# Six first-layer banks by exact parts instead of four, with shared small tiles and a finer written order

## The chip, the cores and the metric

The kernel runs on one core of a Trainium2 chip. The metric is the device time of one execution in microseconds (us). Engines: PE is TensorE, DVE is VectorE, ACT is ScalarE, POOL is GpSimd and SP is SyncE (which here only starts transfers).

## The reference

A gated linear attention with outer-product states (4 batches, 8 heads, 768 tokens, 48 features a head), and behind it a two-layer network with a leaky activation. All in float32.

```python
f = 1.0 / (1.0 + np.exp(-f_logit))
for t in range(S):
    state = f[:, :, t, :, None] * state + np.einsum('bhd,bhe->bhde', k[:, :, t], v[:, :, t])
    y[:, :, t] = np.einsum('bhd,bhde->bhe', q[:, :, t], state)
x = y.transpose(0, 2, 1, 3).reshape(B * S, H * D)      # 3072 x 384
h = x @ w_in                                            # 384 x 2048
g = np.maximum(h, 0.0) + alpha * np.minimum(h, 0.0)
out = g @ w_out                                         # 2048 x 384
```

## The kernel before

**Tiling.** Work goes in 12 steps: 6 chunks of 128 tokens by 2 pairs of sequences. A step holds the attention of two sequences on one chunk and the network of those 256 tokens. The attention of step n+1 runs beside the network of step n.

**Attention of a step.** Transfers bring f, q, k, v (`loaded`, lines L313 and L323; POOL's queue after the first step). ACT takes the sigmoid and copies; DVE makes products of gates inside four-token quads (`lagged_all`, L338 to L345), two scans of 289 columns over the quads' gates (`scanned_all`, L373 and L374), and scaled keys and queries. PE makes three kinds of scores: `raw` inside quads (L582), `qu` between quads of a 32-token block (L591), `off` between blocks (L566). DVE copies the first two under masks into `ad` (`lags` L599 and `quartered` L451), for sequence u = 0 and 1 each; ACT places `ad` into the score matrix A (`placed`, L606). PE then makes py = A and state by v (`summed`, L614), and the state's increments (L539). The scaled keys ks are turned by DVE and two SP transfers through DRAM into ksn (L467, L473, L475). ACT copies py into y, and SP transfers carry y through DRAM into xT, features by tokens (`given`, L503 and L505).

**Network of a step.** The first layer has 8 banks f = 0 to 7, each 256 of the 2048 hidden features by 256 tokens, accumulated in one PSUM bank out of a pool of four. A plain bank is `products(f, w_in, xT)` in float32. From step 3 on, banks 3 to 6 are made by parts: w_in is split once into a high part that a float32r pass multiplies exactly and a low part, xT each step likewise. The bank is then a pass hi by xh and a pass lo by xl (word Na), a scaling copy in place on ACT (Nq, L844), and a third pass sum by xs (Nb). xh is a rounding copy on ACT; xl and xs are copies on ACT that POOL transfers finish by adding (words NY and NZ, L823). Each bank ends in ACT's L854 (Nr) and two DVE instructions L859 (Nc), which write `gate`. The second layer is seven half-size products (Np, L886) of sums of gate blocks (L880) with sums of w_out blocks, as in Strassen's scheme; DVE and ACT add their results into o, SP stores it.

**Parts of w_in.** Per piece of w_in in banks 3 to 6: Y is ACT's high part (L770), Z is DVE's low part and sum (L774, L775), and `turnover` (T) scales the four sums on ACT (L796) once the room of the first pieces is free.

**Order.** Tile pools place buffers and put in the semaphores; the order in which PE, DVE and ACT get their instructions is written by hand in `ORDER_WORDS`: a word is a step number and a part, as `4U0`, and issues all instructions of that part at once. SP's and POOL's instructions are ordered by the framework. Small words: f, F, g, G, h, i, k, l, t are stages of the attention's gates, keys and queries; r and u are the score products, R and U the masked copies, A the placing, y and Y the product py and its copy, X the way to xT, d, D and M the state. Matmuls without use (I, J and the first 14, L935) run in the first step.

The constants: masks `mraw` (four shifted copies) and `mquad`, a 1 and 0 pattern `ones` of 289 columns, the gate row `fs` with its separating ones, `ad` for two sequences, `vs` with 16 spare columns for each sequence's rows.

Of the kernel before, what the change touches and what calls it, by code (L numbers as in the profile page):

```python
# [18 lines left out]
C = 128  # L19
# [16 lines left out]
SPLIT = 3, 7  # L36
TURNED = 3
# [4 lines left out]
0e 1e 0I0 0f 0F 0G 0g 0r1 0h 0i 0m 0p 0j 0r0 0I1 0l 0I2 a0 0R0 0I3 0I4 0I5 0q 0o a1 0k a2 0O 0s 0t w0 0u0 0U0 0R1  # L42
0K0 0H0 1f 0J0 0J1 0J2 w1 0K1 0u1 0J3 0U1 1F 0A0 0d 0D 0H1 0A1 w2 1G 0J4 0J5 0y0 0Y0 b0 0J6 0y1 0x0 0Y1 0M 1g 1i 0J7
1r0 0x1 1R0 0X a3 1h a4 b1 w3 a5 1m 1r1 w4 1j 0Na0 v0 0Nr0 0Na1 0Na2 1R1 0Na3 a6 0Nc0 w5 0Nr1 0Na4 0Na5 0Nc1 2e 0Nr2
1l 1k 0Nr3 a7 0Nc2 1o b2 0Nr4 1K0 1p 1O v1 w6 w7 0Na7 1K1 0Nc3 0Nc4 b3 v2 b4 0Na6 1q 0Nr5 0Nc5 1u0 0Nr6 b5 0Nc6 0Nr7
v3 1u1 1s 2f 1U0 0Nc7 b6 1U1 1H0 1A0 2F 1t 0Np0 v4 0Np1 0Np2 v5 1d b7 v6 V 1H1 1D v7 2g 0Np3 0Np4 1A1 1y0 1y1 1Y0
0Np5 W0 1Y1 1X W1 Y3 W2 0Np6 W3 2G 1Na0 W4 W5 0Np7 0No0 2h 1M 0No1 2i 1Nr0 1Na1 Y4 Y5 1Na3 2p 1Nr1 2q W6 1Na2 1Na4
Y6 3e 1Nr2 2u0 2l 1Nc0 1Nr3 2t 1Nc1 2k 1Nm0 1Nr4 1Nc2 2r0 1Nc3 W7 1Nm1 1Na5 1Nc4 1Na6 1Nr5 2R0 1Nr6 2r1 2U0 2K Z3
2u1 1Nc6 2R1 2A0 1Na7 1Nr7 1Nc5 2o 1Np0 2U1 2O 3f 1Nc7 2d Z4 1Nk 2D 2A1 1Np2 3F 1Np1 2y0 2y1 1Np3 2Y0 2Y1 2X 1Nu0
1Nu1 1Nv0 3G 3g 1Np4 1Nd 1Nv1 1Nw0 1Ng 2M 1Nw1 1Ne 1Nj 1Nh 1Np5 3h 1Np6 1Nf 1Nl 3p 1Ni 3i 1NL 2Na0 3l 4e 2Nr0 2Na1  # L50
2Nr1 2Na3 2Na2 1Ns1 3q 2Nr2 3r0 3u0 2Nc0 2Nr3 3k 3t 2Nc1 2Nm0 3R0 3U0 2Na5 2Nc2 2Nc3 2Nm1 2Na4 Z5 2Nr4 3r1 2Nr5 3K
3u1 2Na7 3R1 2Na6 3o 3A0 2Nc5 2Nr6 2Nc4 3O 3U1 2Nc6 Z6 3A1 3d 3D 2Np0 2Nr7 2Np1 2Nk 2Nc7 4f 2Nd T 3y0 3y1 4F 3Y0
2Np2 1Ns0 3Y1 3M 4g 2Np3 4r0 2Nu1 2Nu0 2Np4 3X 2Nv0 4G 2Nv1 2Nw0 2Ng 3Nx 3Ny 2Nw1 2Ne 2Nj 2Nh 2Np5 4h 2Np6 2Nf 2Nl
4p 3Na1 3Nz 3Na0 4i 3Nr0 2NL 2Ni 4k 4l 3NY 3Na2 4q 3Nr1 3Na7 4K 3Na3 5e 2Ns1 3Nr2 3Nc0 3NZ 3Na4 3Nc2 4t 3Nc1 3Nr7
3Nm0 4u0 3Nc7 4R0 4U0 3Nq3 3Na6 4r1 4A0 4R1 3Na5 4u1 4U1 3Nq4 3Nq5 3Nq6 4o 4O 3Nb3 3Nr3 3Nc3 3Nb4 3Nm1 2Ns0 3Nb6
3Nb5 4d 3Nr4 3Nr5 4D 3Np0 4A1 3Nr6 3Nc6 3Nc5 4y0 3Nc4 4y1 3Np2 5f 4M 4Y0 4Y1 3Np1 3Nk 5F 4X 5g 3Np3 3Nu0 3Nu1 3Nv0
5G 3Nv1 3Nw0 3Ng 3Np4 4Nx 4Ny 3Nw1 3Nd 3Ne 5h 3Nj 3Np5 3Np6 3Nh 3Nf 3Nl 5p 3Ni 5r0 4Nz 4Na0 5i 4Nr0 4Na1 3NL 5k 4NY
4Na5 5l 4Nq5 4Na2 5q 4Nr1 5K 4Na3 4Nc0 4Nr2 5u0 5t 4Nc1 4Nm0 4Nc2 5R0 5U0 4Na7 4Nr7 4NZ 4Na4 6e 3Ns1 5r1 4Nc7 4Nq4
4Nq3 5A0 5u1 5R1 5U1 4Na6 4Nb5 4Nb3 5o 4Nq6 4Nr3 5d 5O 4Nc3 4Nb4 5A1 4Nm1 5D 4Nr4 4Nr5 4Nb6 4Np0 4Nr6 5y0 4Nc4 4Nc5
6f 4Nc6 5y1 5Y0 6F 4Np2 5Y1 5X 6g 4Nk 4Np1 4Np3 4Nu0 4Nu1 4Nv0 4Nv1 4Ng 6G 5Nx 5M 4Nw0 4Np4 5Ny 4Nw1 4Nd 3Ns0 4Ne 6h  # L60
4Nj 4Nh 4Np5 4Nf 4Nl 6p 4Ni 5Nz 5Na0 4Np6 6i 5NY 6k 5Nr0 5Na1 4NL 6l 5Na2 6q 5Na7 5Nr1 6t 5Nc1 6u0 5Nr2 5Nc0 6r0
5Nm0 5Nc2 6R0 5Nr7 5NZ 7e 4Ns1 5Na4 6K 5Na3 6U0 5Nc7 5Na5 6r1 5Nq3 6A0 6u1 6R1 6U1 5Nq4 5Nb3 5Nq5 5Na6 5Nb4 6o 5Nr3
5Nq6 5Nc3 6O 6A1 6d 5Nm1 5Nb6 6D 5Nb5 5Nr4 5Nr5 5Np0 5Nr6 5Nc4 5Nc6 7f 6y0 5Nc5 5Nk 7F 6y1 6Y0 5Np2 6Y1 5Np1 6X 7g
5Np3 5Nu0 5Ng 7G 5Nu1 5Nv0 5Nv1 5Nw1 5Np4 6Nx 5Nw0 5Nd 6M 5Ne 6Ny 7h 5Nj 5Nh 5Np5 5Nf 5Np6 4Ns0 7p 5Ni 6Nz 6Na0 5Nl
7i 7l 6NY 6Nr0 6Na1 5NL 7k 7q 6Na2 6Nr1 7t 6Nc1 6Nr2 6Nc0 6Na7 6Nm0 7K 6Na3 6Nq3 7r0 6Nc2 7u0 7R0 6Nr7 6NZ 6Na4 8e
5Ns1 7U0 6Nc7 6Nq4 6Na5 7u1 7r1 6Nq5 7A0 7R1 7U1 6Na6 6Nq6 6Nb3 6Nr3 6Nc3 6Nb4 6Nm1 6Nb6 6Nb5 7A1 7o 6Nr4 6Nr5 6Nc4
6Nr6 7d 8f 6Np0 7O 6Nc5 7D 6Nk 6Np1 7y0 8F 7y1 6Nc6 7Y0 6Np2 7Y1 7X 8g 7Nx 7M 6Np3 6Nu0 6Nu1 6Np4 6Nv0 6Nd 6Nv1 6Nw0
6Ng 8G 7Ny 6Ne 6Nj 6Nw1 8h 6Nh 6Np5 6Nf 7NY 6Np6 5Ns0 6Nl 8p 6Ni 8i 7Nz 7Na0 7Nr0 7Na1 7Nr1 6NL 8k 8l 7Na2 8t 8r0
7Nr2 7Nc0 8q 7Nc1 8R0 9e 6Ns1 8K 7Na3 7Nm0 7Na7 8u0 7Nc2 7Nr7 7NZ 7Na4 8U0 7Na5 7Nq3 7Nq4 7Nc7 8r1 8u1 7Nq5 8A0 7Na6
8R1 7Nb4 7Nb3 8U1 7Nq6 7Nr3 7Nc3 7Nm1 7Nb6 7Nb5 8o 8A1 8d 7Nr4 7Nr5 7Nc4 7Nr6 8D 8O 9f 7Np0 7Nc5 7Nk 7Np1 7Nc6 8y0  # L70
9F 8y1 8Y0 8Y1 7Np2 8X 9g 7Nd 8M 7Np3 7Nu0 7Nu1 8Nx 7Ne 7Np4 7Nv1 7Ng 9G 8Ny 7Nv0 7Nw0 7Nw1 7Np5 7Nh 9h 7Nf 7Nj 9r0
7Np6 6Ns0 7Nl 9p 7Ni 9R0 8Nz 8Na0 8Na7 9i 8Nr0 8Na1 7NL 9k 9l 8Na2 9q 8Nr1 8NY 8Nr2 9t 8Nc0 8Nc2 8Nc1 8Nr7 8NZ 8Na4
# [11 lines left out]
9Ns0 10Nl 10Ni 11Nz 11NY 11Na0 11Nr0 10NL 11Na2 11Nc0 11Na3 10Ns1 11Nr1 11Nc1 11Nm0 11Nr2 11Nc2 11Nr7 11NZ 11Na4  # L84
11Na5 11Nq3 11Nq4 11Na6 11Nq5 11Nb3 11Nc7 11Nq6 11Nb4 11Nr3 11Nb5 11Nc3 11Nr4 11Nr5 11Nm1 11Nb6 11Np0 11Nc4 11Nr6
11Nc5 11Nc6 11Nk 11Np1 11Np2 11Nd 11Np3 11Nu0 11Nu1 11Nv0 11Nv1 11Np4 11Nw0 11Ng 11Ne 11Nw1 11Np5 11Nj 11Nh 11Np6
10Ns0 11Nl 11Nf 11Ni 11NL 11Ns1 11Ns0
"""

def flat():  # L90
# [924 lines left out]
```

## Time and profile before

| what | value |
|---|---|
| median of three runs | 595.62 us (595.44 to 600.27) |
| profiled execution, first to last instruction (span) | 592.1 us |
| profiled execution's whole time | not listed; the median lies 3.5 us above its span |
| PE busy before 42.7 us | 35.8 us |
| PE busy from 42.7 to 556.7 us | 512.4 of 514.0 us |
| PE busy in the last 35.4 us | 31.9 us |
| one DVE gated product L859, one scaling copy L844 | 0.476 us, 0.574 us |
| one score copy L606 (four for a sequence) | 0.403 us |
| one scan L373 | 0.755 us |
| one high part L770, one low part L774 | 0.84 us, 0.95 us |
| POOL's adding transfers L823, issue to landing | 4.0 us |

The profile's page gives each engine's busy time and share, then forty equal slices in tenths, then the chain of work that ended last. Groups are named by the kernel's line and by output <- inputs. PE's records overlap one another, so the cost of one in a run is its start to the next start. The steps' first layers begin at 188.6 us (step 3), 234.7, 281.7, 324.1, 369.7, 416.2, 461.7 and 506.4 us (step 10).

### The profile page before, as it was taken

What the parts mean: (1) busy time and instruction counts of PE and PEld (TensorE: products, weight loads), DVE (VectorE), ACT (ScalarE), POOL (GpSimd) and SP (SyncE); (2) the same over time, 40 slices, a digit from 0 to 9 for tenths busy, and PEclk for the clock granted to TensorE, in tenths of its full rate; (3) what the DMA queues carried; (4) which work ended last, traced back from release to release, by engine and by line L of the source; (5) the groups of instructions that cost most, each with busy time, mean ns of one, the idle gap of its engine ahead of it and who ended that gap; (6) DMA issues with size and microseconds to landing.
All of it is one profiled execution on the core that took longest, in us unless ns stands there. A gap on an engine that the chain in (4) does not pass through costs nothing.

```text
span 592.1 us, 18853 instructions
## 1 busy us (share of the span) xinstructions
PE 580.1 (98%) x8200; PEld 527.9 (89%) x8200; DVE 505.7 (85%) x1027; ACT 300.4 (51%) x561; POOL 68.4 (12%) x114
## 2 busy tenths in 40 slices
PE   8799999999999999999999999999999999999997
PEld 6678767899899999999999999899899999899997
DVE  7889799899999989899989889989989979966243
ACT  5697973461472473483382374374275355443230
POOL 9110010000101101111111101101100100100100
PEclk9689999999999999999999999999999999999999
DMA  9959212612523823724624614722732731611300
GB/s 299 356 160 348 98 22 63 172 30 86 123 86 91 191 78 89 172 65 105 169 60 106 153 68 106 164 74 85 148 110 81 152 110 54 112 44 30 80 2 27
DMA packets 69443, 67.57 MB, mean 114 GB/s; under 512 B 44688, under 2 KB 58640, under 8 KB 69360
## 3 DMA queue, kind: packets, MB, share of 16 engines
q1 hardware_dynamic: 59744, 37.16, 22.1%
q0 software_dynamic: 8880, 28.84, 19.2%
q8 instruction: 64, 1.05, 0.7%
q10 hardware_dynamic: 736, 0.37, 0.2%
q14 instruction: 19, 0.16, 0.1%
HBM read 44.99 MB, written 13.50 MB: 99 GB/s over the span
## 4 chain that ended last, share of the span: by engine, by line
PE 80%; issue 10%; DMA 4%; ACT 3%; DVE 3%; POOL 1%; POOLq 0%; ACTq 0%; DVEq 0%
PE ph L831 36%; PE pa L886 9%; PE pd L886 5%; PE pf L886 5%; PE pe L886 5%; PE pb L886 5%; PE pc L886 4%; PE py L614 3%; PE qu L591 3%; PE raw L582 3%; DMA w_out_raw<-in_w_out 2%; PE pd L539 1%; PE off L566 1%; DVE ad L451 1%; DMA f<-in_fT 1%
## 5 line engine op out<-in xcount | busy, mean ns | idle before, releaser
L831 PE MATMUL ph<-xT,w_in_sb 128*128 128x256 f32 x612 | 137.1, 380 | 0.2 <-DMA xT<-y 0.2
L831 PEld LDWEIGHTS ph<-xT,w_in_sb 128*128 128x128 f32 x612 | 115.1, 190 | 16.9 <-issue 0.9
L854 ACT ACTIVATE gate<-ph 128x512 f32<-128x512 f32 x96 | 54.6, 594 | 134.4 <-PE ph L831 127.5
L859 DVE SCALAR_TENSOR_TENSOR gate<-gate,om,ph 128x256 f32<-128x256 f32 x192 | 81.0, 476 | 25.6 <-ACT gate L854 25.1
L886 PE MATMUL pa<-w_out_sb,gate 128*128 128x192 f32 x352 | 61.7, 329 | 0.0
L880 DVE TENSOR_TENSOR gate<-gate 128x512 f32<-128x512 f32 x88 | 57.6, 690 | 3.2 <-PE pb L886 2.4
L886 PEld LDWEIGHTS pa<-w_out_sb,gate 128*128 128x128 f32 x352 | 57.1, 190 | 0.5
L599 DVE COPY_PREDICATED ad<-mraw,raw 128x256 f32<-128x256 int32 (+1 forms) x96 | 42.7, 445 | 8.9 <-PE raw L582 6.2
L451 DVE COPY_PREDICATED ad<-mquad,qu 128x224 f32<-128x224 int32 (+6 forms) x140 | 42.2, 302 | 6.8 <-PE qu L591 1.7
L606 ACT COPY A<-ad 32x256 f32<-32x256 f32 x96 | 38.7, 403 | 11.8 <-DVE ad L451 10.4
L440 DVE TENSOR_TENSOR scores<-scores,fs 128x768 f32<-128x768 f32 (+5 forms) x60 | 37.4, 623 | 1.6
L844 ACT ACTIVATE ph<-ph 128x512 f32<-128x512 f32 x36 | 20.2, 574 | 34.0 <-PE ph L831 25.2
L831 PE MATMUL ph<-xh,hi 128*128 128x256 f32 x216 | 34.4, 295 | 0.0
L831 PE MATMUL ph<-xl,lo 128*128 128x256 f32 x216 | 32.0, 283 | 0.3 <-issue 0.3
L886 PE MATMUL pb<-t,gate 128*128 128x192 f32 x176 | 31.2, 331 | 0.0
L831 PEld LDWEIGHTS ph<-xh,hi 128*128 128x128 f32 x216 | 28.7, 190 | 2.8 <-issue 1.6
L424 ACT COPY A<-q 48x512 f32<-48x512 f32 x44 | 27.2, 617 | 7.8 <-DVE q L398 7.2
L886 PE MATMUL pd<-t,gate 128*128 128x192 f32 x176 | 30.7, 328 | 0.3 <-DVE gate L880 0.3
L886 PE MATMUL pc<-t,gate 128*128 128x192 f32 x176 | 30.6, 327 | 0.0
L886 PE MATMUL pf<-w_out_sb,gate 128*128 128x192 f32 x176 | 30.5, 327 | 0.0
L323 POOL DMA_DIRECT2D vs<-in_v x22 | 13.2, 605 | 149.4 <-PE py L614 149.1
L886 PE MATMUL pe<-w_out_sb,gate 128*128 128x192 f32 x176 | 30.4, 326 | 0.0
(153 smaller groups left out, 1044.0 us busy)
## 6 DMA issues: line engine op xcount, KB each, us to landing
w_out_raw<-in_w_out SPq DMA_DIRECT2D x8, 767.8 KB, 9.6
w_in_raw<-in_w_in SPq DMA_DIRECT2D x8, 767.2 KB, 9.5
q<-in_qT POOLq DMA_DIRECT2D x11, 512.0 KB, 5.1
f<-in_fT POOLq DMA_DIRECT2D x11, 512.0 KB, 5.2
k<-in_kT POOLq DMA_DIRECT2D x11, 512.0 KB, 4.2
turned<-f SPq DMA_DIRECT2D x40, 128.0 KB, 4.4
ksn<-turned SPq DMA_DIRECT2D x10, 512.0 KB, 3.5
out<-o SPq DMA_DIRECT2D x24, 192.0 KB, 1.9
```

The source lines that it names most:

```text
L424: nc.scalar.copy(A[halves(cc)[1], :, par * HP:(par + 1) * HP, CH * cc:CH * (cc + 1)], x["q3"][rows(par)].rearrange("p (u h c) s t -> p u h ...
L440: nc.vector.tensor_tensor(by_four(us[:, :, UO[m]:UO[m] + 4 * n]), by_four(us[:, :, skip:skip + 4 * n]), spread(fq[:, :, 1:1 + n], n), ALU. ...
L451: nc.vector.copy_predicated(ad[:, u, :, :, 4 * m:DB], mquad[:, lo:lo + n].bitcast(I32).unsqueeze(1).unsqueeze(1).broadcast_to((128, 2, HP, ...
L582: nc.tensor.matmul(raw[DB * j:DB * (j + 1), par, hp * C:hp * C + QW], lhsT=x["k"][r_, g * DB:(g + 1) * DB], rhs=qd[r_, g], start=True, sto ...
L599: nc.vector.copy_predicated(adu[:, :, :, d:4], mraw[:, d, :, d:4].bitcast(I32).unsqueeze(1).broadcast_to((128, H, NB, n)), rv[:, :, QO[d]: ...
L606: nc.scalar.copy(A[s_, u, :, s_], ad[s_, u].rearrange("p r h t -> p (r h) t"))
L831: nc.tensor.matmul(banks[f][:, j * T:(j + 1) * T], lhsT=of[:, kt, 128 * j:128 * (j + 1)], rhs=by[:, kt], start=first_ and kt + j == 0, sto ...
L844: nc.scalar.activation(banks[f], banks[f], AF.Copy, scale=1.0 - 1.0 / EPS)
L854: nc.scalar.activation(to, of, AF.Relu, scale=-1.0)
L859: nc.vector.scalar_tensor_tensor(to[:, j], to[:, j], om[:, m:m + 1], of[:, j], ALU.mult, ALU.add)
L880: nc.vector.tensor_tensor(block(to)[:, p], block(x_)[:, p], block(y_)[:, p], op)
L886: nc.tensor.matmul(banks[to][:, 0:DH], lhsT=block(of)[:, f], rhs=of_w_out(by)[:, f], start=start and f == 0, stop=f == NH - 1, skip_group_ ...
```

## The change

Banks 2 to 7 are by parts (`SPLIT = 2, 8`), so only banks 0 and 1 stay plain from step 3 on. Parts are now generators: a word issues one instruction, or the run up to the next `yield`, and occurs as often as the part has stretches; the hi and the lo pass are two words as well. The loading word e is four: ef, eq, ek, ev. SP and POOL follow the written order too. The written order is new (1186 words become 2264). Room is made: `mquad` and the shifts in `mraw` go, and the copies take broadcast rows of `inq` and `diag`; `ones` is halved and the scans run in halves; `fs` moves into the q tile from the second chunk on; `ad` holds one sequence (a second one only in the first two steps); ks shares the buffer of ksn and y; the spare columns of `vs` are shared; `ident`, `mhalf` and the first `fs` live in the space freed after loading. The sums of w_in's parts are formed by a DVE word of their own (S), and the low part by an ACT and a DVE instruction (Z).

```diff
-SPLIT = 3, 7
-TURNED = 3
+SPLIT = 2, 8
+TURNED = SPLIT[1] - SPLIT[0]
...
+class Word:
...
+    def __call__(self):
+        if self.left is None:
+            got = self.part()
+            self.left = got if hasattr(got, "gi_frame") else iter(())
+        next(self.left, None)
...
-    ad = const.tile([128, U, 2, HP, DB], F32, tag="ad", name="ad")
+    ad = const.tile([128, 2, HP, DB], F32, tag="ad", name="ad")
     nc.gpsimd.memset(ad, 0.0)
+    ads = ad, stage.tile([128, 2, HP, DB], F32, tag="ad", name="ad_first")
...
+        if c:
+            yield
+            nc.scalar.copy(x["fs"][:, 0:NS:NB + 1], ones[:, 1:2].broadcast_to((128, G + 1)))
...
-        nc.vector.tensor_tensor_scan(ps, fs, ones, 0.0, ALU.mult, ALU.add)
-        nc.vector.tensor_tensor_scan(ss[:, ::-1], fs[:, ::-1], ones[:, ::-1], 0.0, ALU.mult, ALU.add)
+        for half in range(2):
+            if half:
+                yield
+            p = slice(half * HS, half * HS + HS)
+            nc.vector.tensor_tensor_scan(ps[:, p], fs[:, p], ones, 0.0, ALU.mult, ALU.add)
+        for half in range(2):
+            yield
+            p = slice(half * HS, half * HS + HS)
+            nc.vector.tensor_tensor_scan(ss[:, ::-1][:, p], fs[:, 1:NS][:, ::-1][:, p], ones, 0.0, ALU.mult, ALU.add)
...
+            ks=lambda: work.tile([128, GC, 2, DB], F32, tag="ksn", name=f"ks_{i}", bufs=1),
...
+            fs=lambda: x["q"][:, 2 * NS - 2:3 * NS - 2] if c else first_fs,
...
             for m in range(1, NB):
+                if m > 1:
+                    yield
                 lo = UO[m] + (4 if m == 1 else 0)
                 n = DB - 4 * m
-                nc.vector.copy_predicated(
-                    ad[:, u, :, :, 4 * m:DB],
-                    mquad[:, lo:lo + n].bitcast(I32).unsqueeze(1).unsqueeze(1).broadcast_to((128, 2, HP, n)),
-                    x["qu", u][:, :, 0:HP * UW].rearrange("p r (h x) -> p r h x", h=HP)[:, :, :, lo:lo + n])
+                to, of = (t[:, :, at_:at_ + n].rearrange("p h (i r) -> p h i r", r=4) for t, at_ in (
+                    (ad.rearrange("p r h t -> p (r h) t"), 4 * m),
+                    (x["qu", u].rearrange("p r (h x) -> p (r h) x", h=HP), lo)))
+                nc.vector.copy_predicated(to, inq[:, 0:NB - m].bitcast(I32).unsqueeze(1).unsqueeze(3)
+                                          .broadcast_to((128, H, NB - m, 4)), of)
...
     def rest_of_w_in(f):
-        w, hi = piece_of_w_in(f), late["hi"][:, f - SPLIT[0]].bitcast(F32)
-        nc.vector.scalar_tensor_tensor(late["lo"][:, f - SPLIT[0]], hi, 1.0 / EPS, w, ALU.mult, ALU.add)
-        nc.vector.scalar_tensor_tensor(sums[f - SPLIT[0]], hi, 1.0 / EPS - 1.0, w, ALU.mult, ALU.add)
+        hi, lo = (late[n][:, f - SPLIT[0]] for n in ("hi", "lo"))
+        nc.scalar.activation(lo, hi.bitcast(F32), AF.Copy, scale=1.0 / EPS)
+        yield
+        nc.vector.scalar_tensor_tensor(lo, piece_of_w_in(f), 1.0 / EPS, lo.bitcast(F32), ALU.mult, ALU.add)
+
+    def sum_of_w_in(f):
+        hi, lo = (late[n][:, f - SPLIT[0]].bitcast(F32) for n in ("hi", "lo"))
+        nc.vector.tensor_tensor(late["sum"][:, f - SPLIT[0]], lo, hi, ALU.subtract)
...
             if by_parts(f):
                 products(f, late["hi"][:, f - SPLIT[0]], late["xh"], True, False)
+                yield
                 products(f, late["lo"][:, f - SPLIT[0]], late["xl"], False, False)
...
-    with tc.manual_schedule(engines={mybir.EngineType.PE, mybir.EngineType.DVE, mybir.EngineType.Activation}):
+    with tc.manual_schedule(engines={mybir.EngineType.PE, mybir.EngineType.DVE, mybir.EngineType.Activation,
+                                     mybir.EngineType.Pool, mybir.EngineType.SP}):
```

Of the written order, part of step 4 (words of steps 3 to 5), before:

```
3Np1 3Nk 5F 4X 5g 3Np3 3Nu0 3Nu1 3Nv0
5G 3Nv1 3Nw0 3Ng 3Np4 4Nx 4Ny 3Nw1 3Nd 3Ne 5h 3Nj 3Np5 3Np6 3Nh 3Nf 3Nl 5p 3Ni 5r0 4Nz 4Na0 5i 4Nr0 4Na1 3NL 5k 4NY
4Na5 5l 4Nq5 4Na2 5q 4Nr1 5K 4Na3 4Nc0 4Nr2 5u0 5t 4Nc1 4Nm0 4Nc2 5R0 5U0 4Na7 4Nr7 4NZ 4Na4 6e 3Ns1 5r1 4Nc7 4Nq4
```

and after:

```
4U0 3Nc2 3Na3 3Nc2 4U0 4U0 4U0 3Na6 3Na6 4ev 3Na3 3Nr7 4U0 S5 4ev 4A0 4A0 2Ns0 4A0 3Na4 4A0 3Nq3 3Nc7 3Na4 3Nq4 3Nc7
4R1 4R1 3Na5 3Nq6 3Nb3 3Nr3 3Nm0 4l 4R1 3Nc3 3Nc3 3Na5 3Nb6 4R1 4u1 4o 5ev 4t 4t 4O 4O 4O 4l S4 4U1 4U1 4U1 3Nb4 3Nr4
...
3Nw0 3Nu1 3Nw1 3Nv1 5g 5g 5h 5h 3Np6 3Np4 5p 5p 3Ng 5G 5i 5r0 5i 5i 5l 5q 5l 3Np5 4Nx 3Ne 4Ny 4NY 4Nz 5q 4Na1 4Nr1 4M
3Nj 3Nl 3Nf 4Na7 3Ni 5l 3NL 4M 5R0 4M 4Na2 4Na2 3Nh 5t 4Na0 5q 5q 5t 4Nr0 4Nc1 4Nq2 4Na7 4NZ 4Nq7 5u0 4Nb2 5k 5k 5K
5R0 4Nr2 4Na3 4Nb7 4Nc0 4Nc0 3Ns1 4Na3 5t 4Na5 4Na5 5R0 4Nc1 5R0 5U0 5u1 5K 5r1 6ev 4Na4 5l 5l 4Nq5 4Nq3 5K 5K 4Nc2
```

## The prediction

> **What bounds the kernel now.** I read the page's busy rows and slices first, then the busy time by stage, then the chain of work that ended last, then the TensorE timeline inside one step.
>
> ```profile
> span 592.1 us, 18853 instructions
> PE 580.1 (98%) x8200; PEld 527.9 (89%) x8200; DVE 505.7 (85%) x1027; ACT 300.4 (51%) x561; POOL 68.4 (12%) x114
> PE   8799999999999999999999999999999999999997
> DVE  7889799899999989899989889989989979966243
> ```
> TensorE (PE) is at nine tenths or more nearly everywhere; VectorE (DVE) is close behind until the last eighth. ScalarE (ACT) is half idle. Busy time by stage, steps 6, 7 and 8:
>
> ```profile
> 324.10:369.70 45.60, 45.25 (x683) 42.70 (x681) 41.64 (x88) 22.68 (x43) 4.34 (x6) 1.00 0.43 109
> 369.70:416.20 46.50, 46.50 (x745) 43.20 (x744) 42.50 (x90) 22.65 (x43) 5.21 (x7) 1.00 0.45 112
> 416.20:461.70 45.50, 45.47 (x681) 42.47 (x680) 40.89 (x86) 22.54 (x43) 5.23 (x7) 1.00 0.45 109
> ```
> The columns are the stretch, its length, then busy time of PE, its weight loads, DVE, ACT and POOL, and the granted clock (1.00). PE has almost no gap (45.74 of 45.87 us a step in the mean); DVE averages 41.7 us a step, so it has 4.2 us to spare. The chain says the same, and gives the two sizes that matter:
>
> ```profile
> 546.27 2.59 PE ph L831 x12
> 556.65 13.77 PE ph L831 x96
> 570.42 2.60 PE pa L886 x16
> ...
> 586.02 2.61 PE pf L886 x16
> ```
> A first-layer bank in plain float32 is 12 matmul records and takes 2.59 us from start to start. Banks by parts, in the TensorE timeline of step 9:
>
> ```profile
> 475.81 0.98 PE L831 MATMUL ph<-xh,hi 128*128 128x256 f32 x6
> 476.63 0.88 PE L831 MATMUL ph<-xl,lo 128*128 128x256 f32 x6
> 477.35 0.88 PE L831 MATMUL ph<-xs,sum 128*128 128x256 f32 x6
> 478.06 0.88 PE L831 MATMUL ph<-xh,hi 128*128 128x256 f32 x6
> 478.78 0.88 PE L831 MATMUL ph<-xl,lo 128*128 128x256 f32 x6
> 479.50 0.87 PE L831 MATMUL ph<-xs,sum 128*128 128x256 f32 x6
> 480.30 0.92 PE L582 MATMUL raw<-qd,k 48*32 48x80 f32 x64
> ```
> Read start to start, since the durations overlap: a pass is 0.72 us (477.35 - 476.63), so a bank is 3 x 0.72 = 2.16 us. The first pass after other work takes 0.82 us (476.63 - 475.81).
>
> **The change part by part.**
>
> Two more banks by parts. Steps 3 to 11 are nine; 2 x 9 = 18 banks go from 2.59 to 2.16 us: 18 x 0.43 = 7.7 us off PE, all on the path while PE stays the bound. Counting in the two orders, PE enters a run of parts passes 37 times and not 27, since whole banks and attention products now stand between passes. An entry costs 0.10 us by the row above; in other places the pass after a whole bank took up to 0.18. 10 x 0.10 = 1.0 us back (ends 0 and 1.8). PE net: -6.7 us.
>
> In the Trainium skill, "TensorE: Matmul & The Clock Gate", section "Back-to-back issue gap", a 256-column matmul takes 262 cycles at 2.4 GHz, 109 ns. By that estimate six of them take 0.66 us and a bank by parts 1.97 us, and the 18 banks would save 11 us, not 7.7. The trace disagrees: 0.72 us for six, 120 ns each, and it decides.
>
> Scaling copies: 18 more activations on ACT at 0.574 us (L844) are 10.3 us. ACT goes from 22.6 to about 24 us of a 45 us step, so its load is covered; what it costs if the cover is gone is the wait of a third pass. From a bank's second pass to its third there lie one copy and two hand-overs: about 0.9 us. In the new order at least two passes or an attention product (1.4 us or more) stand between wherever I looked (5Na7, 5Nb2, 5Na4, then 5Nb7). Taken at 0; ends 0 and 18 x 0.9 = 16 us.
>
> The input's parts. xh, xl, xs are made as before; the two POOL transfers that finish them land 4.0 us after issue. At 364.69 xT is used first by xh, and the second transfer is issued at 371.36, so xs is whole about 10.7 us after xT. The whole banks ahead of the first third pass fall from four to two, but with the hi and lo passes and the score products between it still starts about 12 us behind the first whole bank, which itself starts 5 us behind xT (369.48 against 364.69). Covered; cost 0.
>
> Preparing two more pieces of w_in. Before: per piece two ACT (0.84) and two DVE instructions (0.95), four pieces. After: the same for six. +3.4 us ACT, +3.8 us DVE, between about 139 and 282 us, where DVE was busy 133.7 of 142.7 us. With it DVE is at 137.5 and PE needs about 141. Taken at 0, worst 2 us.
>
> Scans in halves: 4 a step for 2. A whole one is 0.755 us for 289 columns. The fixed part of a DVE instruction lies near 0.16 us (L451: 0.195 us for 32 elements, 0.407 for 224), so a half is about 0.46 and a pair costs 0.16 more: 0.3 us of DVE a step. It lies beside PE as long as DVE's spare time does not run out: 0.
>
> Masks. The predicated copies for the quads get inner runs of four elements, with a broadcast mask. The nearest row is L599, whose 128x256 form has such runs: 0.444 us, on the line through L451's durations. No change in cost (ends -0.1 and +0.3 us a step, off the path).
>
> One `ad` for two sequences. From here on DVE's first copy for sequence 1 (R1) must wait until ACT has placed sequence 0: four copies (L606), 1.65 us, with hand-overs about 2.0. Queued behind R1 on DVE are the gated products, for which PE's second layer waits. Cover in the new order: between the last 4U0 and 4R1 stand S5 and two 4Nc7, 1.8 us; between 3U0 and 3R1 about 2.9 us; 5: 1.8 us or more. I take 0.1 us a step on DVE, nothing on PE; ends 0 and 4 us a step (both sequences bare).
>
> ks shares its buffer with ksn and y, so DVE's write of ks waits for the transfers that read the last step's y (issued at 357.59, xT whole by 364.69). In most steps two or more microseconds of DVE work, often nine, lie between. In step 11 only 1.6 us do. 0 to 2 us once on DVE; 0 on PE.
>
> fs moves into the q tile: one ACT copy a step (33 columns, below 0.3 us), and q can be loaded again only when the scans' and quads' factors are dead. POOL's q load waited for the same part of the step already (for L418). POOL and SP now follow the written order too. POOL's longest wait was for vs behind py, 149.1 us in all, and PE stood still for none of it; v's load is now a word of its own. Nothing taken; a transfer queued behind such a wait could cost up to 4 us in one step.
>
> Start and end. PE's idle time before 42.7 us is 6.9 us and after its last product 3.5; the first two steps and the tail keep their dependences. Less memory setting on POOL (mquad, mraw) lies beside loads. 0, ends -3 and +3 us.
>
> Sum: -7.7 + 1.0 = -6.7, span 592.1 - 6.7 = 585.4. The median of the runs is 595.62, 3.5 us above the profiled span, for what lies around it; the profiled execution's whole time isn't listed, so I carry the 3.5: 588.9 us.
>
> **The rivals.**
>
> Hand-overs eat half. DVE's spare time falls from 4.2 to about 3.1 us a step (PE a step shorter by 0.74, DVE longer by 0.3 to 0.4), four PSUM banks carry six banks with an ACT round trip, and PE stalls for banks or third passes. At 0.2 us for each of the 18 new banks it is 3.6 us back: 592.5 us. For it: in the list of waits, DVE's gated products stood 25.1 us for ACT and ACT's scaling 25.2 us for PE, so these hand-overs are met just in time. Against: PE idled only 1.6 us in the 514 us between start and tail with 36 such banks.
>
> Finer order gains more. The written order now splits each part into instructions, which lets PE take its gaps out of the middle and start earlier: 1.6 us there and up to 3 at the start: 584.3 us. By the Trainium skill's estimate above it would be 585. Against: the gaps in the middle are nearly nil already.
>
> The single `ad` decides: slower. Place: R1 behind A0, and the next step's R0 behind A1. Bare, each is 2.0 us of DVE waiting, 4.0 a step, over the 3.1 us of spare time; and as the spare time is needed for the waits that DVE already has (waits for ACT and PE), nearly all 4.0 may land on PE: ten steps, 40 us, less 6.7: 629 us. It decides from 0.67 us a step that reaches PE (no gain) and is slower by 1% from about 1.3 us. Some 1.7 us a step, about half a wait, gives 588.9 + 17 = 606 us, which I take as its time. Against: the cover counted above.
>
> **How the numbers follow.** About 1%, 6 us, is what a measurement of this kernel can tell from no change: 589.7 to 601.6 us. Forecast 0.50, of which 0.40 under 589.7. Hand-overs 0.20, within 1%. More gain 0.17, faster. Single `ad` 0.13, slower. So faster 0.57, same 0.30, slower 0.13. The time is that of the likeliest, 588.9 us, with a range of its own of 586.5 to 591.5. The whole range reaches down past the finer order to 583.5 and up over the hand-overs to 598, leaving out most of the 0.13 and about 0.04 below.
>
> **What would show it.** Right: 216 matmul records of each parts pass become 324, plain first-layer records fall from 720 to 504, steps a mean of 0.7 us shorter from step 3 on, PE's busy time near 573 us with idle time near 12. DVE near 512 us. Hand-overs: PE gaps between parts passes put down to L844's scaling or to gated products. Single `ad`: DVE idle ahead of the R copies put down to L606. The prediction is wrong if PE's busy time falls as summed and the span does not, or if the entries into parts passes cost more than 0.2 us each.

## The result, and the profile after

The changed kernel takes 599.71 us in the median of 19 runs (598.41 to 602.81), the kernel before 595.59 us on the same chips (19 runs). The ratio is 1.0073 with a 95% interval of 1.0056 to 1.0089: slower by about 4 us, just under the 1% that the prediction called no change, and 11 us above the forecast. A second set of runs gave 599.82 us and 1.0087 (1.0050 to 1.0125).

The page after: its busy row, and the rows of forty slices for PE and DVE:

```profile
span 601.0 us, 19144 instructions
PE 575.5 (96%) x8308; PEld 526.5 (88%) x8308; DVE 504.1 (84%) x1055; ACT 317.3 (53%) x593; POOL 63.3 (11%) x104
PE   8789999999999999999999999999999989999997
DVE  6878799999889989899989979889889869855252
```

PE's busy time fell by 4.6 us, and the span still grew by 8.9. PE idles 25.5 us where it idled 12.0. DVE's busy time is no higher than before (504.1 for 505.7 us). These two traces show more of a loss than the medians do: the run profiled after is the slowest of its 19 (602.81 us, 1.8 us of it outside the span), while the one before, at some 593.9 us if it has the same 1.8 outside, is among the fastest of its 19. In the medians the loss is 4.1 us, and the second profiled run after has a span of 599.5 us. Busy time from the second layer of step 2 to that of step 11, first in the kernel before, then after (columns as in the prediction's fence):

```profile
166.89:570.26 403.37, 401.98 (x5743) 378.08 (x5737) 347.45 (x723) 198.33 (x373) 41.23 (x55) 1.00 0.41 100
```

```profile
166.85:579.06 412.21, 399.55 (x5974) 378.42 (x5972) 349.06 (x753) 207.59 (x398) 42.53 (x57) 1.00 0.40 99
```

All of the loss is here: 8.8 of 8.9 us. The granted clock rounds to 1.00 in both; after, it falls once for 3.4 us, which the part on the stalls takes up. PE's idle time in the stretch is 1.4 us before and 12.7 after. The first layer's groups (x counts matmul records) after:

```profile
L955 PE MATMUL ph<-xT,w_in_sb 128*128 128x256 f32 x288 | 66.5, 382 | 2.2 <-DVE o L1023 1.6 <-DVE gate L986 0.5
L955 PE MATMUL ph<-xh,hi 128*128 128x256 f32 x324 | 48.9, 290 | 1.2 <-DVE o L1023 1.1
L955 PE MATMUL ph<-xT,w_in_split 128*128 128x256 f32 x216 | 48.7, 382 | 0.1
L955 PE MATMUL ph<-xl,lo 128*128 128x256 f32 x324 | 47.5, 286 | 0.0
L955 PE MATMUL ph<-xs,sum 128*128 128x256 f32 x324 | 45.9, 289 | 0.3 <-DVE sum L906 0.2
```

The counts are those predicted: 324 for each parts pass, 288 + 216 = 504 plain. The passes are as fast as before, in the timeline of step 9:

```profile
476.78 0.98 PE L955 MATMUL ph<-xh,hi 128*128 128x256 f32 x6
477.60 0.88 PE L955 MATMUL ph<-xl,lo 128*128 128x256 f32 x6
478.31 0.88 PE L955 MATMUL ph<-xh,hi 128*128 128x256 f32 x6
479.04 0.84 PE L955 MATMUL ph<-xs,sum 128*128 128x256 f32 x6
```

Start to start 0.82 us for the first pass and 0.71 to 0.73 for the next, as in the kernel before. So the work is what was promised, and the time went into waits. From PE's list of waits (us in total, times, longest), the main ones behind the first step, after:

```profile
PE off L678 <- issue: 4.9, 2, 2.8
PE ph L955 <- DVE o L1023: 2.8, 5, 1.0
PE pc L1013 <- DVE gate L986: 1.0, 1, 1.0
PE off L678 <- DVE ad L560: 0.8, 2, 0.4
PE pb L1013 <- DVE gate L986: 0.7, 2, 0.4
```

In the kernel before, the same list has these put down to nothing, the second of them in the first step, and nothing above 0.3 us put down to DVE behind the first step:

```profile
PE off L566 <- issue: 0.7, 1, 0.7
PE raw L582 <- issue: 0.5, 1, 0.5
```

Two kinds of wait have grown: PE waits for DVE, and PE stands still with no releaser shown ("issue"). The list counts only gaps between records. To count what records hide, each matmul record's start to the next record's start was compared with the steady time of its kind (0.216 us plain, 0.120 in a parts pass, and so on) over everything after 43 us. By that count PE's own work fell by 216 x 0.216 - 324 x 0.120 = 7.8 us, and its lost time rose from about 25 to about 42 us. The sums by cause, in us, for the kernels that follow (good to some 2 us, as they depend on the steady times taken; the differences between kernels are what counts):

| kernel | median, us | ratio to before (95%) | waits for DVE | no releaser, same kind of matmul | change of kind |
|---|---|---|---|---|---|
| before | 595.6 | 1 | 1.0 | 10.1 | 11.8 |
| after | 599.7 | 1.0073 (1.0056 to 1.0089) | 12.2 | 17.8 | 9.2 |
| after, second set | 599.8 | 1.0087 (1.0050 to 1.0125) | 10.5 | 18.9 | 9.7 |
| new order, four banks | 604.8 | 1.0174 (1.0135 to 1.0212) | 11.8 | 11.7 | 10.3 |
| same, own room | 602.2 | 1.0116 (1.0098 to 1.0135) | 11.0 | 9.7 | 9.6 |
| after, urgent first | 596.5 | 1.0017 (0.9995 to 1.0038) | 5.3 | 20.9 | 10.8 |
| after, urgent first, second set | 594.4 | 0.9991 (0.9967 to 1.0016) | 4.1 | 19.0 | 11.0 |
| second set, four banks | 601.9 | 1.0106 (1.0089 to 1.0124) | 7.9 | 15.7 | 10.8 |
| second set, code shifted in a gap | 597.5 | 1.0035 (1.0017 to 1.0054) | 5.8 | 14.9 | 11.1 |
| before, code shifted | 602.4 | 1.0122 (1.0087 to 1.0156) | 1.5 | 15.0 | 11.5 |

The sums are of the one profiled run of each row, so they don't add up to the differences of the medians. Those of after, of "urgent first" and of "second set, four banks" come from the slowest run of their set.

### The profile page after: what moved, and what is told of

The parts are those of the page before. It is cut to its first block, busy times and chain, and to the rows that moved or that the text cites. A ratio compares the mean times of both kernels' runs of the same rounds, so it can differ in the third digit from the quotient of the medians.

```text
span 601.0 us, 19144 instructions
## 1 busy us (share of the span) xinstructions
PE 575.5 (96%) x8308; PEld 526.5 (88%) x8308; DVE 504.1 (84%) x1055; ACT 317.3 (53%) x593; POOL 63.3 (11%) x104
## 4 chain that ended last, share of the span: by engine, by line
PE 57%; DVE 26%; ACT 9%; issue 4%; DMA 3%; SPq 0%; ACTq 0%; DVEq 0%; POOLq 0%
PE ph L955 25%; PE pa L1013 5%; PE pb L1013 3%; PE py L733 3%; PE pc L1013 3%; DVE gate L1007 3%; PE pe L1013 3%; PE po L993 3%; PE pd L1013 3%; DVE scores L544 3%; PE qu L705 2%; PE pf L1013 2%; DVE ad L715 2%; DVE o L1023 2%; DMA f<-in_fT 2%
## 5 line engine op out<-in xcount | busy, mean ns | idle before, releaser
L955 PE MATMUL ph<-xT,w_in_sb 128*128 128x256 f32 x288 | 66.5, 382 | 2.2 <-DVE o L1023 1.6
L955 PEld LDWEIGHTS ph<-xT,w_in_sb 128*128 128x128 f32 x288 | 53.5, 190 | 10.3 <-DVE o L1023 2.8
L955 PE MATMUL ph<-xT,w_in_split 128*128 128x256 f32 x216 | 48.7, 382 | 0.1
L955 PE MATMUL ph<-xl,lo 128*128 128x256 f32 x324 | 47.5, 286 | 0.0
L560 DVE COPY_PREDICATED ad<-inq,qu 128x224 f32<-128x224 int32 (+6 forms) x140 | 42.0, 300 | 6.6 <-PE qu L705 2.8
L955 PE MATMUL ph<-xs,sum 128*128 128x256 f32 x324 | 45.9, 289 | 0.3 <-DVE sum L906 0.2
L969 ACT ACTIVATE ph<-ph 128x512 f32<-128x512 f32 x54 | 30.4, 579 | 29.7 <-PE ph L955 24.6
L955 PEld LDWEIGHTS ph<-xT,w_in_split 128*128 128x128 f32 x216 | 40.5, 190 | 6.0 <-DVE gate L986 0.3
L955 PEld LDWEIGHTS ph<-xl,lo 128*128 128x128 f32 x324 | 42.3, 191 | 0.7 <-issue 0.3
L955 PEld LDWEIGHTS ph<-xs,sum 128*128 128x128 f32 x324 | 41.5, 194 | 1.2 <-ACT ph L969 0.4
L544 DVE TENSOR_TENSOR scores<-scores,q 128x768 f32<-128x768 f32 (+5 forms) x60 | 37.1, 618 | 0.8
## 6 DMA issues: line engine op xcount, KB each, us to landing
w_in_raw<-in_w_in SPq DMA_DIRECT2D x8, 767.2 KB, 10.8
```

The source lines that it names most:

```text
L544: nc.vector.tensor_tensor(by_four(us[:, :, UO[m]:UO[m] + 4 * n]), by_four(us[:, :, skip:skip + 4 * n]), spread(fq[:, :, 1:1 + n], n), ALU. ...
L560: nc.vector.copy_predicated(to, inq[:, 0:NB - m].bitcast(I32).unsqueeze(1).unsqueeze(3) .broadcast_to((128, H, NB - m, 4)), of)
L955: nc.tensor.matmul(banks[f][:, j * T:(j + 1) * T], lhsT=of[:, kt, 128 * j:128 * (j + 1)], rhs=by[:, kt], start=first_ and kt + j == 0, sto ...
L969: nc.scalar.activation(banks[f], banks[f], AF.Copy, scale=EPS - 1.0)
```

## The experiments

**Two banks more, alone.** The changed kernel with four banks by parts, in the new order and the new room.

```diff
-SPLIT = 2, 8
+SPLIT = 3, 7
...
+        order = [key for key in ORDER if key in run]
```

> The changed kernel with SPLIT = 3, 7: four banks by parts again, new order and shared buffers kept, the words of banks 2 and 7 that no longer exist dropped. Theory A (the new order loses more than the two banks bring): PE gets 18 plain banks back at 0.30 to 0.43 us each, so it is slower than the changed kernel, 603 to 608 us. Theory B (the two banks themselves cost, by scaling copies, held PSUM banks and the preparing of two more pieces): faster than the changed kernel, 594 to 598 us. Theory C (the shared buffers cost): near the changed kernel, 599 to 603 us.

Measured: 604.83 us, ratio 1.0174. Against after's 1.0073 the two banks are worth 1.0%, 6 us. The bank arithmetic of the prediction holds in the new order, net of what each program loses to stalls (below); the loss lies in what came with the banks.

**SP and POOL ordered by the framework again.**

```diff
-    with tc.manual_schedule(engines={mybir.EngineType.PE, mybir.EngineType.DVE, mybir.EngineType.Activation,
-                                     mybir.EngineType.Pool, mybir.EngineType.SP}):
+    with tc.manual_schedule(engines={mybir.EngineType.PE, mybir.EngineType.DVE, mybir.EngineType.Activation}):
```

> The changed kernel with the instructions of SP and POOL ordered by the framework again, as before; the rest as changed. Theory A: no change, 598 to 601 us. Theory D (transfers queued in the written order come late: f and ksn are on the chain that ended last): 593 to 597 us.

Measured: 607.64 us, ratio 1.0210 (1.0176 to 1.0244), slower than either theory had it. The written order of these two queues is no loss; in this order it is worth some 8 us. In the trace of this run one third pass waits 4.0 us for ACT's scaling (L969).

**The old order carried over.** Four kernels keep the order of before as a word-by-word translation (all instructions of a part at once, the new words at places of my choice): with six banks, with four, with four and the room of before, and once more with four in the new room. The translation changes part of what is computed, so only their times are used.

```diff
+            while not run[key].ended():
+                run[key]()
```

> Six banks and the shared buffers of the changed kernel in the old written order, whole parts at a word, the two banks' third passes put ahead of their Nr, the placing of sequence 0 moved ahead of R1, SP and POOL ordered by the framework. Theory A: 590 to 595 us. Theory B: 599 us or more. Theory C: 599 us or more.

> As the kernel with six banks in the old order, but with four banks by parts: what is left of the change is the shared buffers, the halved scans and one buffer for the two sequences' scores. Theory A: 594 to 598 us, as before the change. Theory C: 599 us or more. Theory B: 594 to 598 us.

> Old written order, four banks, shared room; the next step's q is loaded only when the gate row that now lies in its tile is done with (the earlier run with this order loaded it too soon, so its output was not the reference's). Theory C: slower than the kernel before by 10 us or more, as in that earlier run (1.03). Theory A: at most 1 to 2 us slower than before.

> Control: the changed kernel's code with the old written order, four banks and unshared room. It should be the kernel before but for how the parts of w_in are prepared and where the POOL transfers of xl and xs stand: 594 to 598 us by every theory. Above 600 us, the old order as carried over here is itself not the old one, and the other runs with it say little.

Measured: 636.92 us (1.0691, 1.0644 to 1.0738), 612.92 (1.0296, 1.0261 to 1.0331), 612.48 (1.0284, 1.0261 to 1.0306) and, with the room of before, 603.49 us (1.0129, 1.0105 to 1.0154). The last is the control, and it should have been at 595 us. A translated order is not the old order, and these runs settle nothing about it. They do show that the shared room costs 9 us under an order that was not made for it.

**What of the loss is room.** The new order and four banks, with two `ad`, ks and fs in tiles of their own, and whole scans; then with two `ad` alone.

```diff
-    ads = ad, stage.tile([128, 2, HP, DB], F32, tag="ad", name="ad_first")
+    ads = ad, const.tile([128, 2, HP, DB], F32, tag="ad_1", name="ad_1")
...
-            ks=lambda: work.tile([128, GC, 2, DB], F32, tag="ksn", name=f"ks_{i}", bufs=1),
+            ks=lambda: work.tile([128, GC, 2, DB], F32, tag="ks", name=f"ks_{i}", bufs=1),
...
-            fs=lambda: x["q"][:, 2 * NS - 2:3 * NS - 2] if c else first_fs,
+            fs=lambda: first_fs,
```

> New order with four banks, and the room not shared: two score buffers for the two sequences, ks and the gate row fs in tiles of their own, whole scans. Against the run with new order, four banks and shared room (1.0174 of the kernel before, about 605 us). Theory A (the order itself loses): stays at 602 us or more. Theory C (the shared room loses, by waits for reused buffers and longer scans): back to 594 to 598 us.

> New order with four banks and shared room, but each of the two sequences has its own score buffer ad. The single-buffer rival of the prediction: 3 us or more faster than with one buffer (602 us or less). Theories A and C without it: 603 to 606 us.

Measured: 602.22 us with all room of its own, 604.68 (1.0161, 1.0141 to 1.0180) with two `ad`. So the new order with four banks and the old room costs 1.2%, 7 us. That price holds the rest of the rewritten code too: how the parts of w_in are made, the masks, the queues of SP and POOL. The translated order with the same code and room cost 1.3%, so no run parts order from code cleanly; that DVE's queue is at the bottom of most of it rests on the next experiment. The shared room costs 0.6% more (1.0174 against 1.0116; the intervals just touch), and the single `ad` some 0.8 us of it, which is within the noise. Order and code +6.9, room +3.4, two banks -6.0: these are differences along one path from the kernel before to the kernel after, so that they add up to the +4.3 us measured is no evidence for any of them. With six banks none of these rooms could be given back; the space does not suffice, so that was not tried.

**Where the order loses: VectorE's queue.** DVE is as busy in both orders (505.7 and 504.1 us), yet PE waits for it 10 to 12 us in the new one and 1.0 in the old. One such place after, step 2's second layer:

```profile
170.73 0.47 DVE L986 SCALAR_TENSOR_TENSOR gate<-gate,om,ph 128x256 f32<-128x256 f32 x1
...
171.13 0.95 DVE L906 TENSOR_TENSOR sum<-lo,hi 128x768 fp32r<-128x768 f32 x1
172.00 0.86 DVE L986 SCALAR_TENSOR_TENSOR gate<-gate,om,ph 128x256 f32<-128x256 f32 x2
...
172.61 0.56 PE L1013 MATMUL pc<-t,gate 128*128 128x192 f32 x2 [0.98 <-DVE gate L986]
```

DVE has both gated products of bank 7 to make (2Nc7, twice), and between them stands S6, a sum of w_in's parts that is not read before step 3's first layer, which starts at 189 us. PE's second layer waits 0.98 us for it. Sixteen such places were mended by moving words; nothing else differs.

```diff
-3U1 2Nr7 3U1 2Nc7 3A1 3A1 3A1 2Np0 2Nk S6 2Nc7 4f
+3U1 2Nr7 3U1 2Nc7 3A1 3A1 3A1 2Np0 2Nk 2Nc7 S7 S6 4f
...
-4p 4G 4q 4h 2Ng 3Nz 3NZ 2Nl 4i 2Nf
+4p 4G 2Nl 2Nf 4q 4h 2Ng 3Nz 3NZ 4i
```

> The changed kernel unedited, for a second trace and a second set of times. In its first trace TensorE stood still twice for over 2 us at the small 48x32 matmuls (2.75 us at 441.9 and 2.15 us at 487.3) with no releaser shown, while a load on GpSimd's queue was in flight; together with smaller ones this made 17.8 us put down to nothing but issue, against 10.1 before. Theory I (such stalls belong to this order and room of code): they come again at the same places, the two together over 4 us, and the span is again near 601. Theory N (they are chance, and the first profiled run, which was the slowest of its 19, was slow because of them): at most one comes again, the issue time falls below 14 us, and the span is 597 to 599. Median time either way 598 to 601, ratio to before 1.005 to 1.010.

> The changed kernel with 21 words of its written order moved, all of VectorE alone: at 16 places an instruction that TensorE was seen waiting for (a gated product that the second layer reads, a sum that frees a bank, the sum of parts that a third pass reads) goes ahead of two to nine instructions that nobody waits for yet, or one of the latter (S6, S7, an m sum, a D piece) goes behind. Nothing else changes: same instructions, same room, same order on the other engines. Theory Q (the new order's loss is in VectorE's queue: 11.4 us of TensorE's waits in the trace are released by VectorE while it works without a gap): the stalls named add up to some 8.5 us, of which a part comes back as later waits; the time falls by 3 to 7 us, to 593 to 597, ratio to before 0.995 to 1.002. Theory L (VectorE's load as such, or the room and the switches between passes, makes the loss, and the order of its queue only chooses which TensorE instruction waits): within 1.5 us of the changed kernel, ratio 1.005 to 1.010.

Measured together: the unchanged kernel 599.82 us (1.0087). Its second trace has one of the two long stalls again (3.04 us at 484.7) and two of 1.2 and 1.5 us elsewhere; the time without a releaser is 18.9 us again. So the sum belongs to the kernel and the single stall varies; neither theory holds whole. With urgent instructions first it is 596.45 us (1.0017, 0.9995 to 1.0038). The same place then:

```profile
166.87 0.87 DVE L986 SCALAR_TENSOR_TENSOR gate<-gate,om,ph 128x256 f32<-128x256 f32 x2 [0.27 <-ACT gate L979]
167.66 1.82 DVE L906 TENSOR_TENSOR sum<-lo,hi 128x768 fp32r<-128x768 f32 x2
...
170.28 0.92 PE L1013 MATMUL pc<-t,gate 128*128 128x192 f32 x4
```

The pair is made at once, both sums follow, and the second layer starts without a wait. A second set of moves, at four more places and without one that had made a wait of its own:

> The changed kernel with a second set of moves in VectorE's written order: those of the kernel with the urgent instructions ahead, but for one that had made a wait of 1.56 us at 199.2 us, and four new ones at the places where its trace still showed TensorE waiting for VectorE (0.2 to 0.5 us each). Theory Q (VectorE's queue order): waits for VectorE fall from 5.3 to about 3 us, the time to 594 to 596, ratio to before 0.997 to 1.001. Theory L: no better than that kernel, ratio 1.001 to 1.005.

Measured: 594.41 us, 0.9991 (0.9967 to 1.0016). Waits for DVE are down from 12.2 to 4.1 us and the time by about 5. Only DVE's words were moved, and the traces show PE's and ACT's instructions in the order they had, so this much of the loss is shown to lie in the order of DVE's queue. By the prices above, that is most of what order and code had cost, and the six-bank kernel now equals the kernel before; it does not beat it. The time without a releaser had not moved, and that was the next question.

**The stalls without a releaser.** The longest stand in the dense small matmuls. The cross products of keys at 487 us, after:

```profile
487.05 0.47 PE L678 MATMUL off<-q,kh 48*32 48x32 f32 x34
489.68 0.45 PE L678 MATMUL off<-q,kh 48*32 48x32 f32 x30 [2.16 <-issue]
```

PE does 34 of 64, stands 2.16 us and goes on. The trace's queue for instructions brings packets of 16 KB, one of them from 487.08 to 488.39 us, just as PE stops. To see whether the place in these packets matters, small unused matmuls were put into the first step of the kernel with the second set of moves; they shift all of PE's later code.

```diff
+    def tiny(to):
+        for _ in range(32):
+            nc.tensor.matmul(to[0:32, 256:288], lhsT=still[0:48, 0:32], rhs=still[0:48, 0:32], start=True, stop=True)
```

> The second set of moves, and 32 extra matmuls of 48x32 into an idle bank in the first step, where TensorE waits for data anyway (about 11 ns each): they change nothing that is used, and shift where TensorE's later instructions stand in the stream that is fetched in packets of 16 KB. Theory F (the long issue stalls in the dense small matmuls, 1.2 to 3.0 us at 264, 398, 441 and 485 us, come where a packet's fetch falls into them): they go, move or change by over 1 us each, while nothing else does; over the three shifts the issue time spreads by over 3 us and the time with it by over 2 us. Theory K (they come from what runs beside them, the load on GpSimd's queue): same places, same lengths, within 1 us in all, whatever the shift.

> As the kernel with 32 extra small matmuls, with 64 (0.7 us of TensorE in the first step). Theory F: the long issue stalls stand elsewhere, or are shorter or longer by over 1 us, than with 32 and without. Theory K: the same places and lengths.

> As the kernel with 32 extra small matmuls, with 96 (1.1 us of TensorE in the first step). Theory F: the long issue stalls stand elsewhere, or are shorter or longer by over 1 us, than with the other shifts; the best of the four beats the kernel before, 590 to 594. Theory K: the same places and lengths, and no time below 594.

Measured: 597.56, 600.72 and 606.77 us. The inserted matmuls took 32 ns a record and not 11, on PE's path: the network's start at 42.7 us came 2.1, 5.8 and 10.2 us later. Of this the matmuls are 2.0, 4.0 and 7.8 us; with 64 and 96 the granted clock was also 0.50 for 3.4 and 10.2 us from 44.1 and 43.1 us on. Less that, the times are 595.5, 594.9 and 596.6, within about 2 us of the unshifted 594.4, and the time without a releaser is 17.9 to 19.2 us in all four: the spread that theory F named is not in the sums. It is in the places. The same products unshifted (with the second set of moves), then with 64 matmuls more:

```profile
482.37 0.47 PE L678 MATMUL off<-q,kh 48*32 48x32 f32 x34
484.88 0.45 PE L678 MATMUL off<-q,kh 48*32 48x32 f32 x30 [2.04 <-issue]
```

```profile
484.23 0.47 PE L678 MATMUL off<-q,kh 48*32 48x32 f32 x34
487.49 0.45 PE L678 MATMUL off<-q,kh 48*32 48x32 f32 x30 [2.79 <-issue]
```

Again 34 and 30. With 32 more matmuls they run through, and another place stops, which runs through in the unshifted kernel:

```profile
211.76 0.58 PE L678 MATMUL off<-q,kh 48*32 48x32 f32 x45
214.54 0.38 PE L678 MATMUL off<-q,kh 48*32 48x32 f32 x19 [2.21 <-issue]
...
485.94 0.75 PE L678 MATMUL off<-q,kh 48*32 48x32 f32 x64 [0.16 <-DVE ad L715]
```

With 96 it is as with 32 (stalls at 220.5 and 360.6 us, the same two matmuls as at 212.1 and 350.3). So the stalls are tied to where the code stands, and a shift by 64 of these matmuls (128 records and their weight loads) is about a whole period.

The packets also show what ends a stop. The trace after has 65 of them, all of 16,384 bytes, for 8308 matmul records and as many weight loads. All 44 stops of over 0.7 us in the 20 traces of this case (41 of them behind the first 43 us) end 1.2 to 1.6 us after a packet's end, whether they lasted 0.7 or 3.5 us. After, the packets ended at 443.55 and 488.39 us, and PE went on at 444.86 and 489.68. Taken in order, the packets pair off with the places 127 records apart where stops are found, and at none of these 1276 places does PE get past sooner than 1.2 us behind its packet's end. So PE stands until its next instructions are there. A stop is long where the packet starts late: the one of 2.94 us at 441.9 us has a packet that started 0.5 us behind PE's last matmul, the one of 0.89 us in the kernel before, at 207.8 us, a packet that started 1.5 us ahead of it.

A stop can cost more than itself. After the second one the clock falls (columns as above, the granted clock third from last):

```profile
491.20:494.60 3.40, 3.40 (x21) 3.17 (x20) 0.52 (x2) 2.64 (x5) 0.00 (x0) 0.50 0.00 0
```

By the steady times this stretch at 0.50 loses some 1.7 us. The second trace after has 6.8 us at 0.50 behind its long stop and loses some 3.2; the kernel before has no such stretch behind its first step. Of the 7.7 us by which the time without a releaser rose, the stops over 0.7 us make 4.4 and the half clock 1.7; in the second trace it is 4.9 and 3.2 of 8.8.

Were the runs before only luckily placed?

> The second set of moves in VectorE's order, with four banks by parts in place of six (the words of banks 2 and 7's parts left out): what the two more banks bring when TensorE waits less for VectorE. Theory G (the two banks bring a fixed 18 bank passes of some 0.30 us each, nearly 6 us, whatever the order): 599.5 to 602, ratio 1.008 to 1.013 against 0.9991 with six. Theory E (the six banks bring issue stalls along, 5 to 7 us in stalls over 0.8 us against 0 to 2 with four, which eat the gain once the order is mended): 595 to 598, ratio 1.000 to 1.005, and its trace shows under 12.5 us of issue stalls against 18 to 19 with six.

> The kernel with the second set of moves and four banks, and the 32 extra small matmuls in the first step, which stand on TensorE's path there (2.2 us in the kernel with six banks). Theory E: the issue stalls stay under 12.5 us with this placement too, so they go with the number of banks. Theory P (four banks had only a lucky placement in the runs so far): stalls over 0.8 us add up to 4 us or more, the issue time to over 15 us. Time: that of the kernel without the shift plus 2 us by theory E, plus 5 to 7 by theory P.

> The kernel before, with the 32 extra small matmuls in its first step, half a packet of 16 KB of TensorE's code. Theory P (the kernel before had a lucky placement): stalls of TensorE over 0.8 us with no releaser add up to 4 us or more against 0.9 in its own trace, the time rises by 5 to 7 us, ratio 1.009 to 1.012. Theory E (they go with the six banks): issue time as before within 2 us (10 to 12), the time rises by the inserted 2.2 us alone, ratio 1.002 to 1.005.

Measured: four banks in the mended order 601.86 us, so the two banks are worth 1.15% there (6.8 us): theory G. Its trace, of its slowest run (606.24 us), has one stall of 3.5 us and 15.7 us without a releaser, more than theory E allows. Shifted, it has three of 1.3 to 2.8 us and takes 614.79 us (1.0315, 1.0290 to 1.0341), 12.9 more in the median, which is beyond theory P as well. Its span is 10.4 us longer: 2.1 are inserted, 4.0 are one wait for an ACT copy at 266 us, and the time without a releaser grew by 5.5. The kernel before, shifted by half a packet, takes 602.43 us, 7.3 more than unshifted, of which 2.2 are inserted. From its list of waits:

```profile
PE raw L582 <- issue: 2.0, 1, 2.0
...
PE qu L591 <- issue: 1.0, 1, 1.0
PE pd L539 <- issue: 0.7, 1, 0.7
```

The time without a releaser is 15.0 us for 10.1, and the stops over 0.7 us are three, 4.5 us, for one of 0.9. Theory P: the kernel before stood well in its packets, by some 5 us, and an edit that shifts PE's code can give that up. The last run tried to choose a place, with 26 extra matmuls in PE's wait at 14.7 us.

> The kernel with the second set of moves and six banks, and 26 extra small matmuls (52 records, 1.7 us at the 33 ns a record that the earlier shifts showed) in the 2.77 us at 14.7 us in which TensorE waits for VectorE, so that they cost no time of their own. The long issue stalls of the traces so far all stand within three matmuls of a multiple of 127 matmul records counted from the start, and the cross products of the keys (48x32) are the stretch that suffers most; with this shift by 52 records only few of those multiples fall into that stretch, where the unshifted kernel has seven. Theory F: the stalls at 261, 392, 436 and 483 us are gone, the issue time falls from 19.0 to 13 to 16 us, the time to 589.5 to 592.5, ratio to before 0.990 to 0.996, which is also faster than either kernel. Theory K (the stalls keep their sum wherever the packets end): 593.5 to 596.5, ratio 0.997 to 1.002.

Measured: 597.50 us, 1.0035 (1.0017 to 1.0054): slower than unshifted and than either theory had it. The stalls after 43 us went as theory F says: the four stalls (7.1 us) are gone, three stand elsewhere (4.2 us, at 212.6, 262.2 and 356.3 us), and the time without a releaser fell from 19.0 to 14.9 us. But the first step got stalls of 2.5 and 1.1 us (at `qu` and at the state's increments, which were not in the count), and PE's waits for ACT rose from 2.6 to 5.8 us. Placement can be moved; with one try it was not made to pay.

## Why the prediction was wrong, step by step

- **Two more banks: -7.7 us of PE's work, -6.7 net.** Right. By steady times the work fell by 7.8 us; with entries and all, two banks are worth 6.0 us in the new order and 6.8 in the mended one, stalls included. Counted without stops, a parts bank takes 2.30 us with its entries against 2.61 plain, and the first layer's 96 banks took 232.4 us after and 239.3 before.
- **Cost of an entry, under 0.2 us.** Right: lost time at a change of kind did not rise (11.8 to 9.2 us).
- **Scaling copies at 0.** Right: PE's lost time put down to L969 is 0.45 us after. The pieces of w_in and the scans in halves cost DVE what was summed: 11.5 us against 7.9 for the pieces, 20.7 against 17.8 for the scans. The masks cost nothing (42.0 against 42.2 us). DVE's busy time, forecast near 512 us, is 504.1, but no work went away: the durations of its records add up to 560.0 us for 553.4, the 6.6 us that were forecast, and they overlap one another more, so the busy time falls.
- **Single `ad` at 0, with a rival at 606 us.** The term was nearly right and the rival is refuted, at least with four banks: two `ad` bring some 0.8 us, within the noise, where the rival had 17.
- **ks and fs in shared room at 0.** Mis-sized: with the scans in halves they cost some 2.6 us (3.4 less the `ad`; by the intervals the 3.4 may be 1 to 6, and one stop of 1.0 us that only the traces with ks and fs in shared room show is in it). Which of the three was not separated.
- **PE stays the bound, covers hold ("all on the path while PE stays the bound").** This is the step that failed. I had looked in the new order for cover of four named waits, and for the rest took DVE's spare time (4.2 us a step) as enough. The spare time did stay. What changed is what DVE does first: in 16 places something that PE waits for stood behind something that it does not. The rival "hand-overs eat half" had the place roughly (gated products) and 3.6 us as its price. Measured, the order and the code written with it cost 6.9 us, PE's waits for DVE rose from 1.0 us to 12.2, and moving DVE's words brought back 3 to 4 us (21 words) and 5 us (the second set). The rival's other sign, waits for the scaling copies, did not show.
- **Code placement.** No step and no rival had it. In its two traces the changed kernel has 4 to 5 us of stops more than the kernel before, whose placement was good by chance, and 1.7 and 3.2 us at half clock behind them. This is no term beside the prices above: each of those compares two programs with a placement of their own, and holds what that made.
- **From span to median.** The 3.5 us are not all "what lies around" the span: the profiled run after has 1.8 us outside it (602.81 - 601.0). The rest, 1.7, is that the run profiled before was faster than its median. The forecast doesn't suffer, as 588.9 is the median less 6.7.

The test named last, "PE's busy time falls as summed and the span does not", is close to what happened: the work fell by 7.8 us, the recorded busy time by 4.6, since part of the waits lies inside records.

What stays open: which part of the 6.9 us is order and which the code written with it, and why a packet of instructions starts late. A load on POOL's queue was in flight at the two stops after; this was not varied.

## What to carry to other kernels

A written order has to be read per engine: for each instruction of the second busiest engine, ask who waits for it and when, and put those that the bound engine needs ahead of those that are only due some day; spare time in the sum doesn't help an instruction that stands third in its queue. When a tuned kernel changes, compare the time with an edit that does nothing but shift its code, as the kernel before lost 5 us to one of those; a difference of 1% between two programs can be that alone. Look in the trace for stops in the middle of equal matmuls, and where the instruction packets lie beside them. And take a change of parts, room and order apart: here differences of +7, +3 and -6 us hid behind one +4.

## What the runs showed of the hardware

- PE stopped for 0.7 to 3.5 us in the middle of runs of equal matmuls, with no releaser shown, at positions that repeat: counted in matmul records from the start, all 44 stops over 0.7 us in 20 traces (one has none) stand 88 to 97 records past a multiple of 127, not at the multiples themselves, as the last run's expectation has it (in the two traces after at records 3775, 5808, 6443 and 7078, to within one record 16, 5 and 5 times 127 apart). They end 1.2 to 1.6 us after a 16 KB packet of instructions has landed. Each record has a weight load beside it, so that is some 254 instructions a period. The Trainium skill, "Runtime: NRT & Kernel Launch", section "Instruction fetch mechanics", has code fetched in blocks of 16 KiB, 256 instructions, and calls the cost of crossing a block's end mostly hidden. The period agrees with it; the cost does not: in runs of 11 ns matmuls it was up to 3.5 us here.
- In four traces with six banks (the two after, and the two with urgent instructions first) the granted clock behind the first step fell to 0.50 six times, for 3.4 or 6.8 us, each time within 2 us of the end of a stop or wait of 1.5 us or more (after the stop at 487.3 us, from 491.2). Not every such stop is followed by one: that at 441.9 us is not. A stretch of 3.4 us cost 1.4 to 1.8 us.
- Inserted 48x32 matmuls, all from one input into one output, took 32 ns a record, where the same shape in the cross products takes 11 ns. Which of input and output does it was not varied.
- The halved scan (144 columns) takes 0.455 us for 0.755 whole (289), so some 0.15 us of a scan do not depend on its length.
- A float32r pass takes 0.120 us a record with its weight load, a plain float32 one 0.216. That the pass is exact on the high part is what the kernel is built on; no run here measures it.
